# Three sums of each chunk's transform formed by accumulating DMAs, and the slab's rows in another order

## The chip, the cores and the metric

The kernel runs on one core of a Trainium2 chip. The metric is the device time of one execution in microseconds, the median of several runs. The engines are TensorE (PE; PEld is its weight load), VectorE (DVE), ScalarE (ACT), GpSimd (POOL) and SyncE (SP), which issues most DMAs. Each engine works through its own queue in order.

## The reference

A batch of 8 sequences of 3072 tokens with 256 channels goes through a convolution by FFT, then through two feed-forward layers over all 24,576 tokens.

```python
# x: (8, 3072, 256), filt_r, filt_i: (1537, 256)
X = np.fft.rfft(x, axis=1)
F = (filt_r + 1j * filt_i)[None, :, :]
y = np.fft.irfft(X * F, n=3072, axis=1)
x = y.reshape(8 * 3072, 256)
h = np.maximum(np.maximum(x @ w1, x @ w2), x @ w3)      # 768 wide
x = h @ w_out
h = x @ w_in                                            # 1024 wide
e = np.exp(h - np.max(h, -1)); sm = e / (np.sum(e, -1) + 1e-09)
solu = h * sm
ln = (solu - mean(solu)) / np.sqrt(var(solu) + 1e-06) * g_ln
return ln @ w_out2
```

## The kernel before

The work has two stages that follow each other. In stage one (to about 1640 us) the first feed-forward layer runs over the tokens of all batches, and beside it the FFT convolution of the batches that come next. In stage two the second layer runs over 192 tiles of 128 tokens; the change touches nothing there but the row number of an output.

Stage one takes 288 steps, written (b, tg, f): 8 batches, 6 groups of 512 tokens, 6 slices of 128 of the hidden layer. A step is `moe(i)`. Its `up` issues 12 matmuls of 512 columns into two PSUM banks named `h` (of four), ScalarE's `hm` (line 789), VectorE's maximum into `h` (791), ScalarE's `hh` (794) and VectorE's remainder `hl` (795). Its `down` issues the 6 matmuls of the step two back (806 to 808). Matmuls in float32r with a high and a low part stand for full precision, hence `hh` and `hl`, `xh` and `xl`.

The transform of a batch's 3072 tokens is split 24 x 128. A chunk `ch` is one half of the channels of one batch; batch 0 is done at the start in another way, and chunks 2 to 15 by a generator, `fft_stream`. A chunk lives in a slab `S[ch]`, 128 partitions (a token's place modulo 128) with 24 rows of 128 channels each, loaded by one SyncE transfer of 1536 KB in `take`. The rows are named (s, a): s one of 8, a one of 3, and stored s-major. The steps of a chunk are

- `dft8`: an 8-point transform over s for all three a, on VectorE, through a scratch tile `scr`;
- `fwd3`: a 3-point transform over a, on VectorE;
- for four groups g of rows: `fwd_in` (twiddles: ScalarE writes T from each row, line 427, 428, and VectorE combines them into U), `middle` (a 128-point transform on TensorE, the product with the filter into M on VectorE, a sum and a difference on GpSimd, line 506 and 508, a swap of halves of the partitions by two SyncE transfers, EO on VectorE) and `inv_out` (back on TensorE, twiddles on ScalarE, V in the slab on VectorE);
- `inv3` and `idft8`: the inverse transforms on VectorE. Then Y is there, and `flip` transposes it for the step that needs it.

What sets the order: the generator is advanced between the steps of `moe`. `tt` and `stt`, through which all this VectorE work goes (lines 274 and 278), add an estimate of 60 + 1.05 per element to `cost`, and after each step the loop advances the stream until `cost` has reached 3080 per step and a lead of 40000. Two more rules bind. `have` drives the stream on where the next tokens need a Y that isn't there. `free(ch)` holds chunk ch back until the last tokens of batch (ch - 5) // 2 have been flipped, since there are five slabs. The order so written is then handed to a scheduler that lays it out engine by engine; each engine keeps that order.

Of the kernel before, what the change touches and what calls it, by code (L numbers as in the profile page):

```python
# [19 lines left out]
P = 128  # L20
# [6 lines left out]

GROUPS = [(2, [15, 7, 23]), (4, [3, 19, 11]), (6, [6, 22, 14]), (0, [0, 12, 8, 20])]
N2_OF = [[(8 * a + 3 * b) % 24 for b in range(8)] for a in range(3)]


# [97 lines left out]
def kernel(ctx: ExitStack, tc: tile.TileContext, x0, xr, ff, tw, dft, first_m,  # L129
# [161 lines left out]
    def take(ch):  # L291
        j = ch % NS
        pool = yp if j in (4, 0) else fc
        S[ch] = pool.tile([P, 8, 3, P], F32, tag=f"s{j}", name="S")
        b, dc = divmod(ch, 2)
        nc.sync.dma_start(S[ch], xr[b - 1, dc])

    def scratch():
        return fc.tile([P, 30, P], F32, tag="scr", name="scr")

    def by3(v):
        return v.rearrange("p (s a) d -> p s a d", a=3)

    def dft8(ch):
        take(ch)
        O = S[ch]
        scr = scratch()
# [12 lines left out]
        yield  # L320
        h = eo[:, 0:2]
        tt(h[:, 0], eo[:, 5], eo[:, 7], ALU.subtract)
        yield
        tt(h[:, 1], eo[:, 5], eo[:, 7], ALU.add)
        yield
        stt(O[:, 2:4], h, C8, eo[:, 4:8:2])
        yield
        stt(O[:, 4:6], h, -C8, eo[:, 4:8:2])
        yield

    def idft8(ch, part=slice(0, 3)):
        b, dc = divmod(ch, 2)
        g = S[ch][:, :, part]
        scr = scratch()
        q, m = by3(scr[:, 0:24])[:, :, part], by3(scr[:, 24:30])[:, :, part]
# [82 lines left out]
    def fwd_in(ch, g):  # L418
# [615 lines left out]
    def down2(i):  # L1034
# [83 lines left out]
def _layout(x, filt_r, filt_i):  # L1118
# [60 lines left out]
```

## Time and profile before

| | |
|---|---|
| median of 3 runs | 2717.51 us (2711.11 to 2720.31) |
| the profiled execution | 2719.01 us, span 2717.2 us |
| TensorE busy | 2647.5 us, 97% |
| VectorE busy | 2256.2 us, 83% |
| ScalarE busy | 1466.7 us, 54% |
| GpSimd busy | 903.7 us, 33% |
| chain that ended last | TensorE 80%, VectorE 12%, DMA 4% |

The shares are means over two stages with different limits. A busy TensorE is not one at its peak, since its matmuls overlap and their ends are modelled; the number of instructions in a stretch tells more. "Idle before" counts the time in which an engine waited, with what released it. A line such as 274 is that of the helper `tt`; tiles and shapes tell the callers apart.

### The profile page before, as it was taken

Reading aid. Unit: us, or ns where it says so; the run is one execution under the profiler, and the core shown is the slowest. Engines: PE = TensorE matmul, PEld = TensorE weight load, DVE = VectorE, ACT = ScalarE, POOL = GpSimd, SP = SyncE. Lnnn points to the kernel's source line nnn. Section 1 sums busy time; section 2 is a strip of 40 time slices with the busy share of each in tenths; the row PEclk is TensorE's granted clock in tenths of the full one; section 3 lists DMA queues with packets and bytes.
Section 4 is the critical chain, followed back from the end, with each engine's and each line's share of the span. In section 5 each row is a group of like instructions: output and inputs, shape, how many; then the busy total and the mean of one; then the engine's idle time right before and its main releaser. Section 6 shows DMA issues by size and latency. Waiting matters only on the chain.

```text
span 2717.2 us, 38005 instructions
## 1 busy us (share of the span) xinstructions
PE 2647.5 (97%) x12096; PEld 2154.2 (79%) x12096; DVE 2256.2 (83%) x3890; ACT 1466.7 (54%) x2806; POOL 903.7 (33%) x1302
## 2 busy tenths in 40 slices
PE   6799999999999999999999999999999999999999
PEld 4478777777777777777788888888888888888888
DVE  4889999999999989989776347878878787888875
ACT  3444344444444444444344335777767777777775
POOL 0011110111110001101110003776776666767675
PEclk7899999999999999999999999999999999999999
DMA  9532323223223224232222103555555555555553
GB/s 290 167 96 75 107 58 118 72 60 118 67 81 121 61 74 119 65 94 78 77 84 87 38 24 104 145 146 151 142 145 147 143 142 138 142 145 145 141 129 90
DMA packets 172634, 300.53 MB, mean 111 GB/s; under 512 B 34289, under 2 KB 102385, under 8 KB 170449
## 3 DMA queue, kind: packets, MB, share of 16 engines
q1 hardware_dynamic: 130608, 246.01, 33.9%
q10 hardware_dynamic: 41824, 52.09, 5.9%
q8 instruction: 95, 1.56, 0.3%
q14 instruction: 107, 0.87, 0.1%
HBM read 97.95 MB, written 56.62 MB: 57 GB/s over the span
## 4 chain that ended last, share of the span: by engine, by line
PE 80%; DVE 12%; DMA 4%; issue 2%; SPq 1%; ACT 0%; POOL 0%; DVEq 0%; ACTq 0%; POOLq 0%
PE h L786 21%; PE h L969 19%; PE p L1038 13%; PE p L1040 7%; PE pf L416 5%; PE o L807 4%; PE o L808 4%; PE o L815 4%; PE o L806 3%; DVE scr L274 2%; DVE S L278 2%; DVE h L791 1%; DVE hl L795 1%; DVE M L274 1%; DVE S L274 1%
## 5 line engine op out<-in xcount | busy, mean ns | idle before, releaser
L1031 POOL TENSOR_TENSOR sl<-zt,sh 128x1024 fp32r<-128x1024 f32 x188 | 453.2, 2411 | 118.5 <-ACT sh L1030 107.8
L274 POOL TENSOR_TENSOR M<-M,M 128x384 f32<-128x384 f32 (+1 forms) x112 | 150.3, 1363 | 848.4 <-DVE M L274 734.9
L1038 PE MATMUL p<-V,sh 128*128 128x512 f32 x1536 | 380.4, 389 | 0.0
L980 DVE SCALAR_TENSOR_TENSOR sp<-h,e 128x1024 f32<-128x1024 f32 x192 | 234.1, 1219 | 159.9 <-ACT e L978 158.0
L794 ACT CAST hh<-h 128x512 fp32r<-128x512 f32 x288 | 169.6, 589 | 306.7 <-DVE h L791 295.4
L1038 PEld LDWEIGHTS p<-V,sh 128*128 128x128 f32 x1536 | 287.3, 188 | 59.3
L789 ACT ACTIVATE hm<-h 128x512 f32<-128x512 f32 x288 | 173.7, 603 | 264.7 <-PE h L786 262.9
L978 ACT ACTIVATE e<-h,sm 128x1024 f32<-128x1024 f32 x192 | 213.8, 1114 | 104.9 <-DVE sm L976 69.1
L976 DVE TENSOR_REDUCE sm<-h 128x1 f32<-128x1024 f32 x192 | 231.3, 1205 | 41.5 <-PE h L969 40.8
L1030 ACT CAST sh<-zt 128x1024 fp32r<-128x1024 f32 x188 | 196.6, 1047 | 114.5 <-PE p L1038 95.7
L982 ACT ACTIVATE e<-sp,sm 128x1024 f32<-128x1024 f32 x192 | 220.5, 1149 | 54.9 <-DVE sm L984 47.1
L791 DVE TENSOR_TENSOR h<-hm,h 128x512 f32<-128x512 f32 x288 | 196.4, 683 | 59.0 <-PE h L786 55.1
L969 PE MATMUL h<-wih,x2h 128*128 128x512 f32 x768 | 243.6, 392 | 1.2 <-ACT xo L818 1.2
L807 PE MATMUL o<-hl,woh 128*128 128x512 f32 x576 | 237.4, 412 | 5.8 <-DVE hl L795 5.8
L969 PE MATMUL h<-wih,x2l 128*128 128x512 f32 x768 | 241.6, 391 | 0.0
L969 PE MATMUL h<-wil,x2h 128*128 128x512 f32 x768 | 238.5, 390 | 0.0
L997 DVE STREAM_TRANSPOSE yt<-sp 128x1024 f32<-128x1024 f32 x188 | 231.4, 1231 | 5.0 <-issue 1.0
L806 PE MATMUL o<-hh,woh 128*128 128x512 f32 x576 | 230.2, 400 | 0.8 <-ACT hh L794 0.8
L795 DVE TENSOR_TENSOR hl<-h,hh 128x512 fp32r<-128x512 f32 x288 | 195.0, 679 | 37.9 <-ACT hh L794 37.8
L808 PE MATMUL o<-hh,wol 128*128 128x512 f32 x576 | 226.1, 393 | 0.0
L1040 PEld LDWEIGHTS p<-V,sl 128*128 128x128 f32 x1536 | 209.7, 190 | 14.9
L1040 PE MATMUL p<-V,sl 128*128 128x256 f32 x1536 | 214.9, 282 | 0.0
(167 smaller groups left out, 5626.1 us busy)
## 6 DMA issues: line engine op xcount, KB each, us to landing
zt<-yt SPq DMA_DIRECT2D x752, 128.0 KB, 2.6
x<-xo SPq DMA_DIRECT2D x96, 256.0 KB, 2.2
x<-x ACTq DMA_DIRECT2D x48, 512.0 KB, 3.6
S<-in_xr_dram SPq DMA_DIRECT2D x14, 1536.0 KB, 7.9
out_dram<-ob ACTq DMA_DIRECT2D x168, 128.0 KB, 2.2
zt<-yt SPq DMA_DIRECT2D x640, 32.0 KB, 1.9
F<-in_ff_dram SPq DMA_DIRECT2D x48, 384.0 KB, 3.4
F<-in_ff_dram SPq DMA_DIRECT2D x16, 512.0 KB, 3.9
```

The costliest lines, as they stand in the source:

```text
L274: return eng.tensor_tensor(o, a, b, op=op)
L786: nc.tensor.matmul(ph[j], wt[:, c, f * P:(f + 1) * P], xt[:, c], start=i == 0, stop=i == 5)
L806: nc.tensor.matmul(po[m], wo_h[:, f, cs], hh, start=f == 0, stop=False)
L807: nc.tensor.matmul(po[m], wo_h[:, f, cs], hl, start=False, stop=False)
L808: nc.tensor.matmul(po[m], wo_l[:, f, cs], hh, start=False, stop=False)
L969: nc.tensor.matmul(h[:, fs], xt[:, c, ts], wt[:, c, fs], start=n == 0, stop=n == 5)
L976: nc.vector.tensor_reduce(sm[:, 0:1], h, axis=AX.X, op=ALU.max, negate=True)
L980: nc.vector.scalar_tensor_tensor(sp, h, 1.0, e, op0=ALU.mult, op1=ALU.mult, accum_out=sm[:, 2:3])
L997: nc.vector.transpose(out=YT[g][:, :, t].rearrange("p j c k -> p c j k"), in_=sp.rearrange("p (c j k) -> p c j k", c=NF2, j=4))
L1031: nc.gpsimd.tensor_tensor(lv, z, hv, op=ALU.subtract)
L1038: nc.tensor.matmul(p, sh[:, c], V2[:, c], start=c == 0, stop=False)
L1040: nc.tensor.matmul(p[:, :D], sl[:, c], V2[:, c, :D], start=False, stop=c == NF2 - 1)
```

## The change

Three sums are no longer VectorE instructions but transfers that add to what lies in the slab, issued from GpSimd's queue by a new helper `add_in`:

- in `dft8`, the sum of rows s = 0 to 3 and 4 to 7 (1536 elements per partition): rows 4 to 7 are read from the input in DRAM a second time and added into rows 0 to 3. VectorE forms the difference first, odd rows and even rows apart, since the transfer overwrites what it reads, then the part that needs only the differences, then the part that needs the sums;
- in `fwd3`, r[:, :, 0] + s (1024 elements): s lies in a tile of its own, `sac`, and is added into the slab's rows a = 0;
- in `inv3`, the same for 768 elements.

The slab is now stored a-major (`t` with 3 x 8 rows, seen as (s, a)), so that the accumulated rows lie side by side, the input is laid out to match, and the eight rows of the 8-point transform stand in another order: the pairs of a group lie at 4, 6, 2 and 0, and the output rows are found through `Y_AT`. In `fwd_in` the row j = 0, on which the transfer lands, is taken last. `idft8` has as many instructions of the same sizes as before. The filter tables keep their order, as the groups keep theirs.

```diff
-GROUPS = [(2, [15, 7, 23]), (4, [3, 19, 11]), (6, [6, 22, 14]), (0, [0, 12, 8, 20])]
+GROUPS = [(4, [15, 7, 23]), (6, [3, 19, 11]), (2, [6, 22, 14]), (0, [0, 12, 8, 20])]
+Y_AT = [0, 2, 4, 6, 5, 7, 1, 3]
...
-        S[ch] = pool.tile([P, 8, 3, P], F32, tag=f"s{j}", name="S")
+        t = pool.tile([P, 3, 8, P], F32, tag=f"s{j}", name="S")
+        S[ch] = t.rearrange("p a s d -> p s a d")
         b, dc = divmod(ch, 2)
-        nc.sync.dma_start(S[ch], xr[b - 1, dc])
+        nc.sync.dma_start(t, xr[b - 1, dc])
 
     def scratch():
-        return fc.tile([P, 30, P], F32, tag="scr", name="scr")
+        return fc.tile([P, 18, P], F32, tag="scr", name="scr")
+
+    def addend():
+        return fc.tile([P, 8, P], F32, tag="sac", name="sac")
+
+    def add_in(o, a):
+        nc.gpsimd.dma_start(o, a, accum_op=ALU.add)
...
     def dft8(ch):
         take(ch)
         O = S[ch]
-        eo, f = by3(scr[:, 0:24]), by3(scr[:, 24:30])
-        tt(eo[:, 0:4], O[:, 0:4], O[:, 4:8], ALU.add)
-        yield
-        tt(eo[:, 4:8], O[:, 0:4], O[:, 4:8], ALU.subtract)
-        yield
-        tt(f[:, 0:2], eo[:, 0:2], eo[:, 2:4], ALU.add)
-        yield
-        tt(O[:, 6:8], eo[:, 0:2], eo[:, 2:4], ALU.subtract)
+        odd, h = by3(scr[:, 0:12]), by3(scr[:, 12:18])
+        tt(odd[:, 2:4], O[:, 1:4:2], O[:, 5:8:2], ALU.subtract)
+        yield
+        tt(odd[:, 0:2], O[:, 0:4:2], O[:, 4:8:2], ALU.subtract)
+        add_in(O[:, 0:4].rearrange("p s a d -> p a s d"), xr[b - 1, dc][:, :, 4:8])
+        yield
+        tt(h[:, 0], odd[:, 2], odd[:, 3], ALU.subtract)
+        yield
+        tt(h[:, 1], odd[:, 2], odd[:, 3], ALU.add)
+        yield
+        stt(two(O[:, 4:6]), two(h), C8, two(odd[:, 0:2]))
+        yield
+        stt(two(O[:, 6:8]), two(h), -C8, two(odd[:, 0:2]))
+        yield
+        f = odd[:, 2:4]
+        tt(f, O[:, 0:2], O[:, 2:4], ALU.add)
+        yield
+        tt(O[:, 2:4], O[:, 0:2], O[:, 2:4], ALU.subtract)
...
@@ fwd3
-        s, d, t = scr[:, 0:8], scr[:, 8:14], scr[:, 14:20]
+        s, d, t = addend(), scr[:, 0:6], scr[:, 6:12]
...
         stt(t, s[:, 2:8], -0.5, r[:, 2:8, 0])
-        yield
-        tt(r[:, :, 0], r[:, :, 0], s, ALU.add)
+        add_in(r[:, :, 0], s)
         yield
...
@@ inv3
-        s, d, t, t0 = scr[:, 0:6], scr[:, 6:12], scr[:, 12:18], scr[:, 18:20]
+        s, d, t, t0 = addend()[:, 0:6], scr[:, 0:6], scr[:, 6:12], scr[:, 12:14]
         tt(s, v[:, 2:8, 1], v[:, 2:8, 2], ALU.add)
         yield
+        stt(t, s, -0.5, v[:, 2:8, 0])
+        add_in(v[:, 2:8, 0], s)
+        yield
         tt(d, v[:, 2:8, 1], v[:, 2:8, 2], ALU.subtract)
-        yield
-        stt(t, s, -0.5, v[:, 2:8, 0])
-        yield
-        tt(v[:, 2:8, 0], v[:, 2:8, 0], s, ALU.add)
         yield
...
@@ fwd_in
-            for j, k in enumerate(ks):
+            for j, k in order(ks):
...
+    def order(ks):
+        return list(enumerate(ks))[1:] + [(0, ks[0])]
```

How the order of instructions changes shows best at chunk 5, the first that meets a full load of VectorE. VectorE before, from the two instructions of 1536 (sum and difference) that open its `dft8`:

```order
L274 TENSOR_TENSOR scr<-S 128x1536 x2
L791 TENSOR_TENSOR h<-hm,h 128x512
L274 TENSOR_TENSOR M_2289<-Z,F 128x768
L274 TENSOR_TENSOR M_2274<-swap,F 128x768
L274 TENSOR_TENSOR scr<-scr 128x768
L791 TENSOR_TENSOR h<-hm,h 128x512
L274 TENSOR_TENSOR S<-scr 128x768
L278 SCALAR_TENSOR_TENSOR S<-pf,tws,T_2281 128x2x128 x3
L795 TENSOR_TENSOR hl<-h,hh 128x512
L770 TENSOR_TENSOR xl<-h,xh 128x512
L274 TENSOR_TENSOR S<-scr 128x384 x2
L770 TENSOR_TENSOR xl<-h,xh 128x512
```

VectorE now, from the product that stands ahead to the first reader of the accumulated rows, the last `scr<-S` (f); line 805 is the maximum `h`, 809 the remainder `hl`, 275 and 279 the helpers, 784 `xl`:

```order
L275 TENSOR_TENSOR M_2586<-Z,F 128x1024
L275 TENSOR_TENSOR scr<-S 128x2x3x128 x2
L275 TENSOR_TENSOR M_2541<-swap,F 128x1024
L809 TENSOR_TENSOR hl<-h,hh 128x512
L805 TENSOR_TENSOR h<-hm,h 128x512
L275 TENSOR_TENSOR scr<-scr 128x3x128 x2
L279 SCALAR_TENSOR_TENSOR S<-pf,tws,T_2577 128x256 x3
L279 SCALAR_TENSOR_TENSOR S<-scr 128x3x256 x2
L784 TENSOR_TENSOR xl<-h,xh 128x512
L809 TENSOR_TENSOR hl<-h,hh 128x512
L275 TENSOR_TENSOR scr<-S 128x2x3x128
```

The two of 1536 have become two of 768; the sums' part of the transform, which came right behind them, now stands behind the differences' part and behind work of other steps. GpSimd before, from the end of that chunk's neighbourhood on; M1 and M2 are the products of `middle`, S the slabs by number:

```order
L274 TENSOR_TENSOR M1_2915<-M1_2915,M2_2871 128x384 x2
L274 TENSOR_TENSOR M1_3153<-M1_3153,M2_3107 128x384 x2
L274 TENSOR_TENSOR M1_3299<-M1_3299,M2_3284 128x384 x2
L274 TENSOR_TENSOR M1_3440<-M1_3440,M2_3425 128x512 x2
L274 TENSOR_TENSOR M1_3682<-M1_3682,M2_3606 128x384 x2
L437 MEMSET U_3908 128x128
L274 TENSOR_TENSOR M1_3834<-M1_3834,M2_3782 128x384 x2
```

GpSimd now, a similar piece; 307 is `add_in`:

```order
L275 TENSOR_TENSOR M1_2776<-M1_2776,M2_2738 128x384 x2
L307 DMA S_1454<-sac_2694 128x768
L275 TENSOR_TENSOR M1_3021<-M1_3021,M2_2973 128x384 x2
L275 TENSOR_TENSOR M1_3198<-M1_3198,M2_3183 128x384 x2
L307 DMA S_2446<-sac_2981 128x1024
L275 TENSOR_TENSOR M1_3306<-M1_3306,M2_3258 128x512 x2
L307 DMA S_2384<-sac_3398 128x768
L275 TENSOR_TENSOR M1_3519<-M1_3519,M2_3480 128x384 x2
L448 MEMSET U_3781 128x128
L275 TENSOR_TENSOR M1_3669<-M1_3669,M2_3623 128x384 x2
L307 DMA S_4041<-in_xr_dram 128x3x512
```

Three transfers per chunk stand between the pairs, in one queue with them. ScalarE before, at the twiddles of chunk 5's group 0 (T from S_2376; 789 is `hm`, 794 `hh`):

```order
L789 ACTIVATE hm_2717<-h_2703 128x512
L794 CAST hh_2689<-h_2673 128x512
L428 ACTIVATE T_2528<-S_2376,tws_135 128x128
L427 ACTIVATE T_2528<-S_2376,tws_135 128x128 x2
L428 ACTIVATE T_2528<-S_2376,tws_135 128x128
L427 ACTIVATE T_2528<-S_2376,tws_135 128x128
L428 ACTIVATE T_2528<-S_2376,tws_135 128x128
```

ScalarE now (S_2384; 803 is `hm`, 808 `hh`):

```order
L439 ACTIVATE T_2438<-S_2384,tws_135 128x128
L438 ACTIVATE T_2438<-S_2384,tws_135 128x128 x2
L439 ACTIVATE T_2438<-S_2384,tws_135 128x128
L803 ACTIVATE hm_2910<-h_2896 128x512
L808 CAST hh_2873<-h_2857 128x512
L438 ACTIVATE T_2438<-S_2384,tws_135 128x128
L439 ACTIVATE T_2438<-S_2384,tws_135 128x128
L803 ACTIVATE hm_2951<-h_2937 128x512
L808 CAST hh_2913<-h_2897 128x512
L438 ACTIVATE T_2685<-S_2384,tws_135 128x128
```

The twiddles of row 0, the last 438 and 439 of T_2438, come behind a step's `hm` and `hh`, and the next step's stand behind them.

## Rows read from the trace of the kernel before

**Rows 1.** Stretches of the run; columns as the first line names them.

```profile
core 0: us, PE busy (x) PEld busy (x) DVE busy (x) ACT busy (x) POOL busy (x), PEclk, DMA share, GB/s
300.00:380.00 80.00, 73.40 (x296) 55.84 (x295) 75.86 (x125) 32.93 (x81) 7.97 (x6) 0.96 0.33 100
380.00:500.00 120.00, 118.50 (x497) 92.92 (x496) 118.94 (x203) 53.16 (x128) 16.54 (x14) 1.00 0.34 101
500.00:580.00 80.00, 74.77 (x304) 58.01 (x303) 80.00 (x127) 33.75 (x82) 8.36 (x7) 0.96 0.21 58
580.00:1220.00 640.00, 633.48 (x2655) 497.56 (x2655) 611.98 (x983) 290.60 (x694) 77.05 (x63) 1.00 0.31 88
1220.00:1380.00 160.00, 160.00 (x676) 126.47 (x675) 144.05 (x237) 69.22 (x164) 17.44 (x15) 1.00 0.25 69
1380.00:1500.00 120.00, 120.00 (x530) 99.09 (x529) 73.81 (x125) 54.16 (x94) 16.88 (x12) 1.00 0.32 96
```

**Rows 2.** Chain that ended last, around 300 us: start us, us, what.

```profile
...
300.27 11.98 DMA S<-in_xr_dram
...
313.45 0.60 SPq L746
...
322.27 1.15 DVE EO L278 x2
...
```

**Rows 3.** VectorE in order of time, around 330 us: start us, busy us, instruction.

```profile
329.87 3.40 DVE L274 TENSOR_TENSOR scr<-S 128x1536 f32<-128x1536 f32 x2
333.19 0.68 DVE L791 TENSOR_TENSOR h<-hm,h 128x512 f32<-128x512 f32 x1
333.79 0.95 DVE L274 TENSOR_TENSOR M<-Z,F 128x768 f32<-128x768 f32 x1
334.65 0.95 DVE L274 TENSOR_TENSOR M<-swap,F 128x768 f32<-128x768 f32 x1
...
338.06 1.26 DVE L278 SCALAR_TENSOR_TENSOR S<-pf,tws,T 128x256 f32<-128x256 f32 x3
...
342.57 1.01 DVE L274 TENSOR_TENSOR scr<-scr 128x384 f32<-128x384 f32 x2
...
344.56 1.81 DVE L278 SCALAR_TENSOR_TENSOR S<-scr 128x768 f32<-128x768 f32 x2
```

**Rows 4.** VectorE by line and shape, 136 to 1650 us: busy us, mean ns.

```profile
L274 DVE TENSOR_TENSOR scr<-S 128x768 f32<-128x768 f32 x63 | 61.0, 985 | 0.0
...
L274 DVE TENSOR_TENSOR scr<-S 128x1536 f32<-128x1536 f32 x26 | 46.5, 1827 | 1.8 <-DMA S<-in_xr_dram 1.8
...
L274 DVE TENSOR_TENSOR M<-Z,F 128x1024 f32<-128x1024 f32 x14 | 17.0, 1212 | 0.1
```

**Rows 5.** VectorE by line and shape: 300 to 580 us, then 580 to 1220.

```profile
L274 DVE TENSOR_TENSOR scr<-S 128x1536 f32<-128x1536 f32 x8 | 14.7, 1879 | 0.0
L274 DVE TENSOR_TENSOR S<-S,scr 128x1024 f32<-128x1024 f32 x3 | 3.6, 1210 | 0.0
L274 DVE TENSOR_TENSOR S<-S,scr 128x768 f32<-128x768 f32 x3 | 2.8, 942 | 0.0
...
L274 DVE TENSOR_TENSOR scr<-S 128x1536 f32<-128x1536 f32 x12 | 21.5, 1832 | 0.0
L274 DVE TENSOR_TENSOR S<-S,scr 128x1024 f32<-128x1024 f32 x7 | 8.5, 1209 | 0.0
L274 DVE TENSOR_TENSOR S<-S,scr 128x768 f32<-128x768 f32 x7 | 6.6, 947 | 0.0
```

**Rows 6.** DMA issues: out<-in, queue, count, KB each, median us to landing.

```profile
S<-in_xr_dram SPq DMA_DIRECT2D x14, 1536.0 KB, 7.9
...
F<-in_ff_dram SPq DMA_DIRECT2D x16, 512.0 KB, 3.9
...
xb<-in_x_dram SPq DMA_DIRECT2D x1, 1152.0 KB, 13.3
```

**Rows 7.** GpSimd by line and shape, 136 to 1650 us: busy us, mean ns, idle before.

```profile
L274 POOL TENSOR_TENSOR M<-M,M 128x384 f32<-128x384 f32 x84 | 111.1, 1344 | 590.2 <-DVE M L274 508.3 <-ACT hm L789 65.4 <-ACT hh L794 16.5
```

More of the change, by code (lines that the diff above doesn't have):

```diff
@@ L293, in take, with two @@
         pool = yp if j in (4, 0) else fc
-        S[ch] = pool.tile([P, 8, 3, P], F32, tag=f"s{j}", name="S")
+        t = pool.tile([P, 3, 8, P], F32, tag=f"s{j}", name="S")
+        S[ch] = t.rearrange("p a s d -> p s a d")
         b, dc = divmod(ch, 2)
-        nc.sync.dma_start(S[ch], xr[b - 1, dc])
+        nc.sync.dma_start(t, xr[b - 1, dc])
     def scratch():
-        return fc.tile([P, 30, P], F32, tag="scr", name="scr")
+        return fc.tile([P, 18, P], F32, tag="scr", name="scr")
[3 more added lines that the diff above has]
+        nc.gpsimd.dma_start(o, a, accum_op=ALU.add)
     def by3(v):
-        return v.rearrange("p (s a) d -> p s a d", a=3)
+        return v.rearrange("p (a s) d -> p s a d", a=3)
+    def two(v):
+        return v.rearrange("p s a d -> p a s d")
     def dft8(ch):
@@ L306, in dft8 @@
         O = S[ch]
+        b, dc = divmod(ch, 2)
         scr = scratch()
-        eo, f = by3(scr[:, 0:24]), by3(scr[:, 24:30])
-        tt(eo[:, 0:4], O[:, 0:4], O[:, 4:8], ALU.add)
+        odd, h = by3(scr[:, 0:12]), by3(scr[:, 12:18])
+        tt(odd[:, 2:4], O[:, 1:4:2], O[:, 5:8:2], ALU.subtract)
         yield
-        tt(eo[:, 4:8], O[:, 0:4], O[:, 4:8], ALU.subtract)
+        tt(odd[:, 0:2], O[:, 0:4:2], O[:, 4:8:2], ALU.subtract)
+        add_in(O[:, 0:4].rearrange("p s a d -> p a s d"), xr[b - 1, dc][:, :, 4:8])
         yield
-        tt(f[:, 0:2], eo[:, 0:2], eo[:, 2:4], ALU.add)
+        tt(h[:, 0], odd[:, 2], odd[:, 3], ALU.subtract)
         yield
-        tt(O[:, 6:8], eo[:, 0:2], eo[:, 2:4], ALU.subtract)
+        tt(h[:, 1], odd[:, 2], odd[:, 3], ALU.add)
[8 more added lines that the diff above has]
+        tt(O[:, 2:4], O[:, 0:2], O[:, 2:4], ALU.subtract)
         yield
@@ L320, in dft8 @@
         yield
-        h = eo[:, 0:2]
-        tt(h[:, 0], eo[:, 5], eo[:, 7], ALU.subtract)
-        yield
-        tt(h[:, 1], eo[:, 5], eo[:, 7], ALU.add)
-        yield
-        stt(O[:, 2:4], h, C8, eo[:, 4:8:2])
-        yield
-        stt(O[:, 4:6], h, -C8, eo[:, 4:8:2])
-        yield
     def idft8(ch, part=slice(0, 3)):
@@ L334, in idft8 @@
         scr = scratch()
-        q, m = by3(scr[:, 0:24])[:, :, part], by3(scr[:, 24:30])[:, :, part]
+        w, m = by3(scr[:, 0:12])[:, :, part], by3(scr[:, 12:18])[:, :, part]
         tt(m[:, 0], g[:, 0], g[:, 1], ALU.add)
@@ L339, in idft8 @@
         yield
-        tt(q[:, 0:2], m[:, 0:2], g[:, 6:8], ALU.add)
+        tt(w[:, 0:4:2], m, g[:, 2:4], ALU.add)
         yield
-        tt(q[:, 2:4], m[:, 0:2], g[:, 6:8], ALU.subtract)
+        tt(w[:, 1:4:2], m, g[:, 2:4], ALU.subtract)
         yield
-        tt(m[:, 0:2], g[:, 2:4], g[:, 4:6], ALU.subtract)
+        tt(m, g[:, 4:6], g[:, 6:8], ALU.subtract)
         yield
-        tt(q[:, 4:6], g[:, 2:4], g[:, 4:6], ALU.add)
+        tt(g[:, 4:6], g[:, 4:6], g[:, 6:8], ALU.add)
         yield
-        tt(q[:, 6], m[:, 0], m[:, 1], ALU.add)
+        tt(g[:, 6], m[:, 0], m[:, 1], ALU.add)
         yield
-        tt(q[:, 7], m[:, 1], m[:, 0], ALU.subtract)
+        tt(g[:, 7], m[:, 1], m[:, 0], ALU.subtract)
         yield
-        tt(g[:, 0:4:2], q[:, 0:4:2], q[:, 4:6], ALU.add)
+        tt(g[:, 0:2], w[:, 0:2], g[:, 4:6], ALU.add)
         yield
-        tt(g[:, 4:8:2], q[:, 0:4:2], q[:, 4:6], ALU.subtract)
+        tt(g[:, 2:4], w[:, 0:2], g[:, 4:6], ALU.subtract)
         yield
-        stt(g[:, 1:4:2], q[:, 6:8], C8, q[:, 1:4:2])
+        stt(two(g[:, 4:6]), two(g[:, 6:8]), -C8, two(w[:, 2:4]))
         yield
-        stt(g[:, 5:8:2], q[:, 6:8], -C8, q[:, 1:4:2])
+        stt(two(g[:, 6:8]), two(g[:, 6:8]), C8, two(w[:, 2:4]))
         for a in range(3)[part]:
@@ L428, in fwd_in @@
                 nc.scalar.activation(T[:, 2 * j + 1], x[:, 0], AF.Copy, scale=col("ns", k))
-            for j, k in enumerate(ks):
+            for j, k in order(ks):
                 stt(U[:, j:j + 4:3], X[:, sl:sl + 2, j], col("c", k), T[:, 2 * j:2 * j + 2])
@@ L1055, in down2 @@
         a, hf = divmod(tg, 2)
-        row = b * SEQ + N2_OF[a][hf * 4 + j] * P
+        row = b * SEQ + N2_OF[a][Y_AT[hf * 4 + j]] * P
         nc.scalar.dma_start(out[row:row + P], ob)
@@ L1122, in _layout @@
     xr = x[1:].reshape(B - 1, N2, P, 2, P)[:, order]
-    xr = xr.reshape(B - 1, 3, 8, P, 2, P).transpose(0, 4, 3, 2, 1, 5)
+    xr = xr.reshape(B - 1, 3, 8, P, 2, P).transpose(0, 4, 3, 1, 2, 5)
     xr = np.ascontiguousarray(xr)
```

1 line of the change is left out of this document (removed).

## The prediction

> **What bounds the kernel now.** I read the stretches of the whole run first. The reader is to see in [rows 1] that TensorE is busy nearly all the time from 300 us on, and that its instruction count tells more than its busy time: from 1220 to 1380 it gets through 676 matmuls in 160 us, 4.225 per us, with no idle time and with the transform's matmuls still among them. I take that as TensorE's own pace. At that pace 300 to 580 us (three rows, 280 us) would hold 1183 matmuls; the rows hold 296 + 497 + 304 = 1097, so 86 are missing, 86 / 4.225 = 20.4 us. 580 to 1220 would hold 2704 and holds 2655: 49 missing, 11.6 us. What TensorE lost there is the most that a lighter VectorE can give back: 32 us. From 1220 on there is nothing to win: TensorE is never idle there while VectorE is at 144.05 of 160 us and then, from 1380, at 73.81 of 120; the last stage, after it, has TensorE busy throughout in the page's slices as well.
>
> The same rows name the other side. VectorE is busy 274.8 of 280 us in 300 to 580, and 611.98 of 640 in 580 to 1220. So the first of these stretches is VectorE's, with TensorE close behind, and the second is nearly balanced. In the two worst slices the granted clock of TensorE also falls, to 0.96, which is a mean over its two levels of 2.4 and 1.2 GHz; a filled gap would win that back too, and the count above holds it already.
>
> Not all of the loss is VectorE's work. The chain around 300 us [rows 2] runs through the 1536 KB load of a slab, which took 11.98 us there, and through SyncE's queue, where each small transfer behind it takes 0.6 us to issue, to a swap that released the EO step only at 322 us. No VectorE instruction that is taken away here would shorten that.
>
> **What the change removes.** Per chunk, three sums leave VectorE. In dft8 two instructions of 1536 elements become two of 768: the pair took 3.32 us from its start to the start of what follows (329.87 to 333.19), and one of 768 takes 0.86 (333.79 to 334.65) [rows 3], so 3.32 - 2 x 0.865 = 1.59 us go. I use starts and not the mean durations of [rows 4] (1827 and 985 ns), because neighbours overlap by about 0.08 us. In fwd3 a sum of 1024 goes, 1210 ns less that overlap, 1.13 us; in inv3 one of 768, 942 ns, 0.87 us [rows 5]. Together 3.59 us per chunk and 14 chunks.
>
> Does the pace table take it back? The emission loop counts estimated VectorE cost, and the change lowers a chunk's count. But a slab comes free only when the tokens of an earlier batch are flipped, and in the orders of both kernels the chunks start at nearly the same steps (counted by the rows of h that stand ahead in VectorE's order: chunk 5 at step 33 before and 34 now, the last at 200 and 199). So the same transform work still belongs to the same steps, and the load per step falls. By [rows 5] the stretch from 300 to 580 holds 4 dft8, 3 fwd3 and 3 inv3: 4 x 1.59 + 3 x 1.13 + 3 x 0.87 = 12.4 us leave VectorE. The one from 580 to 1220 holds 6, 7 and 7: 23.5 us.
>
> **What it adds.** Each removed sum becomes an accumulating transfer on GpSimd's queue, and its reader must wait for the landing. The trace has no such transfer, so I bound it. From below: 768 KB as a plain load lies between 512 KB at 3.9 us and 1536 KB at 7.9 us [rows 6], 4.9 us. From above: the slowest comparable load, 1152 KB at 13.3 us beside other loads. I take 7.9 us: a sum has two operands, so 768 KB of result means 1536 KB to be read, and that is the slab load's row; with 0.6 us for the issue, as a row of SyncE's queue shows, 8.5 us.
>
> The Trainium skill, "Collectives: The Full Stack", section "The bandwidth ceiling: the fold count and why AG ≠ RS ≠ AR", speaks against the change in the same way: a reducing transfer reads two sources through one ring and delivers about half of what a copy does. By that rule the sum stays at the 7.9 us row; without it, it would be 4.9 us. No run here shows an accumulating transfer yet.
>
> Against it stands the cover. In dft8 of chunk 5 the first reader of the accumulated rows (the sum f) stands behind these instructions after the second subtraction: a product of 1024 (1.13 us), hl and h (0.6 each), two of 384 (1.01 for the pair, less the overlap 0.93), three of 256 (1.18), two of 768 (1.73), xl and hl (0.6 each, like h), 7.4 us by [rows 3, 4]. 8.5 - 7.4 leaves VectorE waiting 1.1 us per chunk; behind the waiting f in its queue stand xl, EO, h and hl, for which TensorE waits if it lasts longer than the two steps of lead that four PSUM banks give. Other chunks have a similar cover, the last two some 2 to 3 us less. The bounds give a wait of 0 (landing after 5.5 us) to 6.5 us (13.9 us).
>
> The second transfer (fwd3, 512 KB) is waited for first by ScalarE: the twiddle of row 0, moved behind the two other rows. It blocks hm and hh behind it in ScalarE's queue. By the same doubling it lands like 1024 KB, between 3.9 and 7.9, say 5.9 us plus the issue, and VectorE reads what depends on it 6.8 us of its own work later at the nearest place. ScalarE is busy 53.16 of 120 us [rows 1], so I cost it at nothing; without that cover it would be the same few us per chunk. The third (inv3, 384 KB) is read by idft8 behind six own instructions and what is interleaved, over 10 us, or frees the shared addend, which is written 5.5 us later or more: nothing. GpSimd's own pairs of sums are unchanged (1344 ns each [rows 7]), and it sat idle 590 us before them; in its new order no transfer stands ahead of a pair that is ready earlier, so issuing costs nothing, at worst one pair's 1.4 us of delay to a swap. The second reading of half a slab and the two transfers inside SBUF add traffic to DMA engines that are busy a third of the time [rows 1]: nothing, or a few tenths per swap. The new row order leaves the number and size of all other VectorE instructions alone. A 768 that reads strided rows costs 985 ns, one that does not 947 [rows 4, 5]: up to 45 ns either way on some dozen instructions a chunk, 0.5 us per chunk, taken as nothing and kept in the range.
>
> **The sum.** From 300 to 580 VectorE is relieved of 12.4 us and given 4 x 1.1 of waiting: 8.0 us net. As it is the bound in most of that stretch, but not in the chain of [rows 2], I count two thirds, 5.3 us. From 580 to 1220 it is 23.5 - 6 x 1.1 = 16.9 us, of which I count a third, 5.6 us, half of what TensorE lost there. Before 300 and after 1220 nothing. Together 11 us: 2719.0 us, the profiled execution, becomes 2708. The median of the runs lies 1.5 us under that execution, so I predict 2707 us.
>
> **Rivals.**
> 1. *The transfer is slow and becomes the wait.* If it lands at the upper bound, 13.9 us after the subtraction, VectorE stands 6.5 us per dft8: 4 x 6.5 - 12.4 = +14 us in the first stretch, all on the path, and 6 x 6.5 - 23.5 = +15 in the second, against 28 us of idle VectorE, so half, +8. 2719 + 22 = 2741. It decides from a landing of 7.4 + 12.4 / 4 = 10.5 us on. For it: slab loads have taken up to 11.98 us, and pairs of them are issued back to back just where the sums start. Against it: the median of 7.9.
> 2. *The removed work is not what TensorE lacked.* If the two gaps come from slab loads and SyncE's queue, as the chain at 300 us shows, less work only makes VectorE wait longer for the same releases: a gain of 0 to 6 us, 2716. Against it: VectorE is busy 80.00 of 80 us from 500 to 580.
> 3. *Everything hides.* If the sum lands like a plain load, no wait appears, and the stretches give 12.4 and at most 11.6 us: 2695. For it: only a third of the DMA time is in use.
> 4. *The change does not take the load off*, since a planner orders anew, and queues (SyncE's above all) come out differently in places: plus or minus 5 us around any of these, inside the ranges.
>
> **Chances and range.** Forecast (gain of 8 to 20 us) 0.37; everything hides 0.09; no difference 0.27; slow transfer 0.27. A measurement of this kernel tells 0.3% from no change, 8 us. That gives faster 0.45, within 0.3% 0.29, slower 0.26. The likeliest case has 2698 to 2711 as its own range. With the other cases it reaches from 2693 (rival 3 against the median) to 2739 (rival 1 against the median).
>
> **What would show it.** Right: VectorE's busy time falls by 14 x 3.6, about 50 us; the rows of 1536 and the sums S<-S,scr are gone; the wait of dft8's f for a transfer is around 1 us each; from 300 to 580 the matmul count rises above 1097 and its clock above 0.96. The forecast is wrong if the landing of the 768 KB transfer is over 10.5 us or ScalarE's twiddle waits hold up hm; then VectorE's idle time grows under a DMA releaser and the counts fall. It is wrong the other way if the 580 to 1220 stretch reaches TensorE's own pace.

## The result and the profile after

The changed kernel takes 2731.98 us (median of 5 runs, 2728.92 to 2733.11) against 2715.86 for the kernel before (2711.11 to 2720.31): ratio 1.0057, 95% interval 1.0043 to 1.0072. It is 16 us slower, where 11 us of gain were forecast. The profiled span is 2731.0 us.

The stretches of the changed kernel, in the columns of [rows 1], which they answer:

```profile
300.00:380.00 80.00, 75.25 (x324) 58.88 (x323) 74.08 (x123) 31.65 (x76) 10.19 (x9) 0.98 0.46 122
380.00:500.00 120.00, 120.00 (x505) 94.31 (x504) 117.86 (x209) 55.22 (x135) 19.05 (x17) 1.00 0.42 114
500.00:580.00 80.00, 73.06 (x298) 55.83 (x297) 75.97 (x125) 34.43 (x87) 14.01 (x12) 0.98 0.39 87
580.00:1220.00 640.00, 630.78 (x2637) 493.97 (x2636) 586.07 (x976) 288.56 (x693) 100.48 (x85) 1.00 0.40 105
1220.00:1380.00 160.00, 156.46 (x657) 122.61 (x656) 132.54 (x217) 65.35 (x153) 17.21 (x17) 1.00 0.33 86
1380.00:1500.00 120.00, 118.60 (x521) 97.13 (x520) 71.56 (x121) 52.16 (x90) 15.83 (x12) 1.00 0.29 88
```

VectorE is lighter in every row, by 12 of 160 us even from 1220 to 1380, and TensorE gets through fewer matmuls in four of the six: 657 for 676 from 1220 to 1380, where the prediction had nothing to be won. Only 300 to 500 gained. Over the whole span VectorE's busy time fell from 2256.2 to 2203.0 us, as forecast. So the load left VectorE, and the time went up.

How a wait travels is seen at the last chunk's dft8, the longest of eight such waits. VectorE in order of time (start, busy, instruction, and in brackets the idle time ahead of it), answering [rows 3]:

```profile
1230.18 1.81 DVE L275 TENSOR_TENSOR scr<-S 128x768 f32<-128x768 f32 x2
1231.92 0.69 DVE L805 TENSOR_TENSOR h<-hm,h 128x512 f32<-128x512 f32 x1
1232.51 1.02 DVE L275 TENSOR_TENSOR scr<-scr 128x384 f32<-128x384 f32 x2
1233.45 0.69 DVE L809 TENSOR_TENSOR hl<-h,hh 128x512 fp32r<-128x512 f32 x1
1234.05 1.82 DVE L279 SCALAR_TENSOR_TENSOR S<-scr 128x768 f32<-128x768 f32 x2
1241.29 0.96 DVE L275 TENSOR_TENSOR scr<-S 128x768 f32<-128x768 f32 x1 [5.42 <-DMA S<-in_xr_dram]
1242.16 1.29 DVE L774 TENSOR_TENSOR xl<-zt,xh 128x512 fp32r<-128x512 f32 x2
1243.37 0.95 DVE L275 TENSOR_TENSOR S<-S 128x768 f32<-128x768 f32 x1
1244.24 0.69 DVE L805 TENSOR_TENSOR h<-hm,h 128x512 f32<-128x512 f32 x1
```

The two subtractions of 768 end at 1232; f, which reads the landed sum, stands behind six more instructions and starts at 1241.29 after 5.42 us of waiting. The h of the MoE step stands behind f. Its wait goes on to ScalarE and from there to TensorE, in the same view:

```profile
1244.96 0.58 ACT L808 CAST hh<-h 128x512 fp32r<-128x512 f32 x1 [6.56 <-DVE h L805]
...
1245.60 0.50 PE L820 MATMUL o<-hh,woh 128*128 128x512 f32 x1 [1.10 <-ACT hh L808]
```

TensorE still had other matmuls to run while f waited, so it stood still for 1.10 us at this place, not for 5.42.

The chain that ended last runs through this transfer here (start us, us, what), as the chain of [rows 2] ran through a slab load:

```profile
1232.30 8.97 DMA S<-in_xr_dram
...
1241.29 0.03 DVE scr L275
```

The transfers of the changed kernel (KB each, median us to landing), answering [rows 6]:

```profile
S<-in_xr_dram SPq DMA_DIRECT2D x14, 1536.0 KB, 7.4
...
F<-in_ff_dram SPq DMA_DIRECT2D x16, 512.0 KB, 4.3
...
S<-in_xr_dram POOLq DMA_DIRECT2D x14, 768.0 KB, 8.5
...
S<-sac POOLq DMA_DIRECT2D x14, 512.0 KB, 5.6
S<-sac POOLq DMA_DIRECT2D x14, 384.0 KB, 4.1
```

And who waited for them, by the line that issues all three (us in all, times), with VectorE's group of that shape ([rows 4]):

```profile
  ACT T L438: 28.7, 14
  DVE scr L275: 21.1, 8
  DVE sac L275: 2.3, 1
```

```profile
L275 DVE TENSOR_TENSOR scr<-S 128x768 f32<-128x768 f32 x77 | 75.4, 994 | 26.5 <-DMA S<-in_xr_dram 26.5
```

GpSimd's own pairs of sums hardly changed, 1263 ns where [rows 7] have 1344:

```profile
L275 POOL TENSOR_TENSOR M<-M,M 128x384 f32<-128x384 f32 x84 | 104.4, 1263 | 474.6 <-DVE M L275 453.1 <-ACT T L572 10.8 <-ACT th L244 7.4
```

VectorE waited 26.5 us for slabs in front of that shape, 21.1 of them in 8 waits for the accumulating transfer; ScalarE's twiddles (T) waited 28.7 us in 14.

### The profile page after: what moved, and what is told of

It is laid out like the page before. It is cut to its first block, busy times and chain, and to the rows that moved or that the text cites. A ratio compares the mean times of both kernels' runs of the same rounds, so it can differ in the third digit from the quotient of the medians.

```text
span 2731.0 us, 38141 instructions
## 1 busy us (share of the span) xinstructions
PE 2649.9 (97%) x12096; PEld 2151.9 (79%) x12096; DVE 2203.0 (81%) x3862; ACT 1462.9 (54%) x2806; POOL 939.7 (34%) x1344
## 4 chain that ended last, share of the span: by engine, by line
PE 51%; DMA 1%; DVE 1%; SPq 1%; issue 0%; POOL 0%; ACT 0%; DVEq 0%; ACTq 0%; POOLq 0%
PE h L983 19%; PE p L1052 13%; PE h L800 7%; PE p L1054 7%; PE o L829 1%; PE o L821 1%; PE o L822 1%; PE o L820 1%; SPq L760 1%; PE pf L427 0%; DMA raw<-in_w_in_dram 0%; DMA S<-in_xr_dram 0%; DMA raw<-in_w_out_dram 0%; DVE h L805 0%; DMA zt<-yt 0%
## 5 line engine op out<-in xcount | busy, mean ns | idle before, releaser
L994 DVE SCALAR_TENSOR_TENSOR sp<-h,e 128x1024 f32<-128x1024 f32 x192 | 234.2, 1220 | 159.7 <-ACT e L992 157.8
L1011 DVE STREAM_TRANSPOSE yt<-sp 128x1024 f32<-128x1024 f32 x188 | 231.5, 1232 | 4.2
```

Source lines behind the costliest of these rows:

```text
L994: nc.vector.scalar_tensor_tensor(sp, h, 1.0, e, op0=ALU.mult, op1=ALU.mult, accum_out=sm[:, 2:3])
L1011: nc.vector.transpose(out=YT[g][:, :, t].rearrange("p j c k -> p c j k"), in_=sp.rearrange("p (c j k) -> p c j k", c=NF2, j=4))
```

## The experiments

Theory 1: the price is f's wait for dft8's transfer, at the head of VectorE's queue. Theory 2: it is ScalarE's wait for the two others. Theory 3: it is the added traffic. Theory 4: it is the new row order and the new order of instructions. "Layout kernel" means the changed kernel with all three sums on VectorE. The brackets hold the 95% interval of the ratio to the kernel before, run in turn on the same chip.

### Each part alone

```
e1  - add_in(O[:, 0:4]..., xr...)          + tt(O[:, 0:4], O[:, 0:4], O[:, 4:8], ALU.add)
e2  - add_in(r[:, :, 0], s)                + tt(r[:, :, 0], r[:, :, 0], s, ALU.add)
    - add_in(v[:, 2:8, 0], s)              + tt(v[:, 2:8, 0], v[:, 2:8, 0], s, ALU.add)
e3  both of these
e6  e3, with add_in(v[:, 2:8, 0], s) kept
```

Dft8's sum back on VectorE (e1): 

> The changed kernel with the sum of dft8 back on VectorE (one instruction of 1536 elements, in place); the accumulating transfers of fwd3 and inv3 stay, and so does the new row order. Before 2716, changed 2732. Theory 1 (the wait of f for the 768 KB landing, 21 us in 8 waits at the head of VectorE's queue with h and hl behind it, is what costs): most of the 16 us comes back, 2714 to 2720, and VectorE's waits for S<-in_xr are gone. Theory 2 (the 512 and 384 KB transfers cost, by ScalarE's 28.7 us of waiting for them in front of the twiddles): 2728 or more, ScalarE's waits unchanged. Theory 4 (row order and re-planned order alone): 2728 or more as well, told from theory 2 by the layout kernel.

Measured 2709.88 [0.9973, 0.9991], 22 us under the changed kernel and below theory 1's range; theories 2 and 4 expected 2728 or more. VectorE still waits 5.0 us for S<-in_xr, for the slab loads themselves.

Only dft8's as a transfer (e2): 

> The counterpart: only dft8's sum is an accumulating transfer, those of fwd3 and inv3 are on VectorE. Theory 1: 2726 to 2736, as slow as the changed kernel, waits for S<-in_xr of 15 to 25 us on VectorE. Theory 2: 2712 to 2720, ScalarE's waits for S<-sac gone. Theory 3 (the added traffic delays the swaps, EO and M wait 17 us longer in all): in between, since 768 of the 1664 KB per chunk remain.

Measured 2717.36 [1.0004, 1.0022]; VectorE waits 16.8 us for that transfer in 9 waits. The waits are those of theory 1, but the time lies in theory 2's range: measured against the kernel before, this run speaks against theory 1. The next run shows why that was the wrong yardstick.

No transfer (e3): 

> Row order and layout of the changed kernel, but all three sums on VectorE: no accumulating transfer at all. Theories 1, 2 and 3: about before, 2712 to 2722, VectorE's busy time back to 2250 to 2256 us. Theory 4 (the new row order and the re-planned queues cost by themselves): 2728 or more.

Measured 2703.82 [0.9948, 0.9973], VectorE's busy time 2252.3 us. Every theory missed this: the layout alone, which relieves VectorE of next to nothing (before has 2256.2), is 11 us faster than before. Measured from it, the transfers cost far more than 16 us: fwd3's and inv3's 6, dft8's 13.5, all three 28.

Only inv3's as a transfer (e6): 

> The layout kernel (2704) with only inv3's sum as an accumulating transfer (384 KB); dft8 and fwd3 on VectorE. Its reader stands over 10 us later. If a hidden transfer is free and VectorE's relief (14 x 0.87 = 12 us) counts for something: 2698 to 2703. If the relief is worth nothing: 2702 to 2706. If each transfer costs by the way it delays others (theory 3) or by the re-planned order: 2706 to 2712.

Measured 2708.73 [0.9970, 0.9987], 5 us over the layout kernel. That is in the size of what another order of the same work moves (below), so it shows no more than that the 12 us of relief did not appear.

### The transfer itself, in an unchanged order

The next three kernels have every instruction of every engine where the changed kernel has it; only the adding is taken from a transfer, so that it lands sooner.

```
e5   - nc.gpsimd.dma_start(o, a, accum_op=ALU.add)   + nc.gpsimd.dma_start(o, a)
e10  the same in dft8 alone          e11  the same in fwd3 and inv3 alone
```

All three plain (e5): 

> The changed kernel with its three transfers as plain copies to the same places on the same queue, nothing added (the three sums are left out of the result); every instruction of every engine stands where it stood. If an accumulating transfer reads two sources and pays for both, the plain 768 KB lands in 5 to 6 us and not in 8.5; then f hardly waits (under 8 us in all), and by theory 1 the time falls from 2732 to 2712 to 2720. If the landing stays at 8 us or more, adding is free and the time stays at 2728 to 2734. If the landing shrinks and the time doesn't, the waits for transfers are not what costs, and the order is.

Measured 2709.29 [0.9970, 0.9988], below theory 1's range. VectorE's waits for dft8's transfer fell from 21.1 us to 5.6. The landings of e5:

```profile
S<-in_xr_dram POOLq DMA_DIRECT2D x14, 768.0 KB, 5.8
...
S<-sac POOLq DMA_DIRECT2D x14, 512.0 KB, 3.2
S<-sac POOLq DMA_DIRECT2D x14, 384.0 KB, 2.7
```

Only dft8's plain (e10): 

> The changed kernel (2732) in its own order; only dft8's transfer is a plain copy (its sum is left out), those of fwd3 and inv3 still add. With all three plain it was 2709, 23 us less: f's waits fell by 15.1 us, ScalarE's T waits by 19.2. Theory 1 (f's wait is the price): 15 to 22 us less, 2710 to 2717. Theory 2 (ScalarE's T wait is the price): 0 to 8 us less, 2724 to 2732.

Measured 2713.80 [0.9984, 1.0002]: 18 of the 23 us. VectorE's waits for this transfer fell from 21.1 us to 6.3, while its waits for slabs in all fell from 26.5 to 12.3. The last chunk of e10, VectorE in order of time, in the columns of the same place above:

```profile
1219.91 1.82 DVE L279 SCALAR_TENSOR_TENSOR S<-scr 128x768 f32<-128x768 f32 x2
1224.46 0.96 DVE L275 TENSOR_TENSOR scr<-S 128x768 f32<-128x768 f32 x1 [2.72 <-DMA S<-in_xr_dram]
```

The same f, behind the same instructions, waits 2.72 us and not 5.42.

Only the two others plain (e11): 

> The counterpart in the same order: dft8's transfer adds, the two others are plain copies (their sums are left out). Theory 1: 0 to 8 us less, 2724 to 2732. Theory 2: 15 to 22 us less, 2710 to 2717. If both cost: the two gains sum to about 23.

Measured 2730.97 [1.0041, 1.0066]: 1 us. Theory 2 falls as the main price, and with it ScalarE's longer list of waits: ScalarE waited 19 us less, and the time hardly moved. Theory 1 holds for most of the 23 us. Over e10, e5 is another 4.5 us faster, so the two small transfers seem to cost something only once the large one no longer does; with different chips under the two runs, that is not certain.

### The reader later

```
e4   def dft8: f and the three behind it become dft8b, which stages() runs after idft8 of the
     chunk before; else: with tc.issue_after(HL[-3]): tt(f, O[:, 0:2], O[:, 2:4], ALU.add)
```

> All three transfers as in the changed kernel, but the readers of dft8's landed rows (f and what follows) stand later in VectorE's order: behind idft8 of the chunk before where the order allows it (some 50 us of own work between trigger and f), else behind the hl of a later MoE step (10.9 us or more of own work, from chunk 8 on; chunks 5 and 7 keep 6.9 and 6.6). Theory 1: the waits for S<-in_xr fall from 26 us to under 8, and the time to 2716 to 2724. Theory 2 and theory 3: the waits fall too, but the time stays at 2728 to 2734. If later rows only push the chunk's next steps late, it is above 2732.

Measured 2710.75 [0.9977, 0.9995], with 11.1 us of waiting for S<-in_xr instead of 26.5 (theory 1 said under 8); 6.0 of them are for the transfer. The direction is theory 1's; the gain, 21 us, is more than it forecast, presumably since the edit also gives everything around f another order. Even so it stays 7 us over the layout kernel: a transfer that is mostly hidden still did not beat having none.

### Traffic without a reader

```
e8   e3 + nc.gpsimd.dma_start(SPARE[:, :n], xr[b - 1, dc][:, 0, :n], accum_op=ALU.add)   (3 places)
```

> The layout kernel (2704), all sums on VectorE, with three accumulating transfers per chunk issued at the same places (512, 512 and 384 KB from HBM) into a spare tile that nobody reads: traffic and GpSimd issues without any wait for them. Theory 3 (traffic delays swaps and loads): EO's wait for swaps rises from 11.5 to 20 us or more, and the time to 2710 to 2718. Theory 1 (only waits for the landing cost): 2702 to 2706.

Measured 2790.42 [1.0264, 1.0292], and it tells nothing of theory 3. With nothing to wait for, the 42 transfers were all issued by 295 us, and as they share one tile, GpSimd waited for its own. Which work that held up, and so where the 75 us come from, was not followed (us, times, longest):

```profile
POOL spare L316 <- DMA spare<-in_xr_dram: 231.2, 40, 11.8
```

Theory 3 has better evidence against it elsewhere. EO's waits for a swap were 25.0 us in the changed kernel and 24.1 in e5, with nothing added in the transfers and 23 us less time. These waits are longer than the layout kernel's 11.5, but e12 (below), which has no such transfer at all and the same work on VectorE, has 22.8: they come with a lighter VectorE, and the traffic isn't needed for them. The swap<-M itself lands in 3.0 us (median) in the changed kernel and in 2.9 in the layout kernel.

### The order, and what relief is worth

```
e9   before, PACE 3080 -> 3050               e13  e3, PACE 3050
e12  the changed kernel without the three add_in (sums left out)       e18  e12, PACE 3050
e14  e3, the odd half as tt(odd, O[:, 0:4], O[:, 4:8], ALU.subtract)
e15  e3, s = scr[:, 18:26] of one scratch of 26 rows                   e19  e15, PACE 3050
e16  e3, f and the three behind it ahead of h
```

The pace of the kernel before (e9): 

> A control: the kernel before with the pace of its emission loop at 3050 instead of 3080, which gives VectorE, ScalarE and TensorE another order (some 500 to 900 rows differ) and changes no work. If a re-planned order alone moves the time by several us, it shows here: theory 4 says 2705 to 2725, at least 5 us from 2715. If orders of the same work are alike: 2713 to 2718.

Measured 2717.49 [1.0003, 1.0021]: 3 us by order alone.

The pace of the layout kernel (e13): 

> A second control: the layout kernel (2704) with the pace at 3050 instead of 3080. If the layout's gain of 11 us is its own, the time stays at 2701 to 2708; if it is one lucky order of many, it goes to 2709 to 2718.

Measured 2704.90 [0.9946, 0.9970]: the layout's 11 us hold in a second order.

No sums at all (e12, then e18 in a second order): 

> The changed kernel with the three sums neither on VectorE nor as transfers: they are left out. It shows the most that relieving VectorE of them can bring, 53 us of its busy time, without any price. If VectorE's load is what TensorE lacked (the prediction): 2685 to 2697, since TensorE's counts of the layout kernel (2704) leave 78 matmuls or 18 us to win between 300 and 1220. If the relief is worth nothing (rival 2 of the prediction): 2700 to 2710.

Measured 2705.66 [0.9952, 0.9972], which reads as no worth at all. 

> The kernel without the three sums (they are left out; 2706 at a pace of 3080) in another order, at a pace of 3050. If relieving VectorE of 53 us is worth nothing over the layout kernel (2704 and 2705 at the two paces), and 2706 was no unlucky order: 2700 to 2710. If it hid a gain: 2688 to 2698.

Measured 2692.84 [0.9899, 0.9926]. This turns e12's verdict round. Two orders of the same work are 13 us apart. In the slower one TensorE has three waits of over 2 us for hl, which the other hasn't (start, busy, and in brackets the wait; the execution shown took 2710 us, 5 us over the median):

```profile
336.57 0.74 PE L797 MATMUL h<-xh,w0h 128*128 128x512 f32 x2 [2.14 <-DVE hl L806]
...
530.49 1.22 PE L797 MATMUL h<-xh,w0h 128*128 128x512 f32 x2 [3.39 <-DVE hl L806]
...
1054.54 0.67 PE L818 MATMUL o<-hl,woh 128*128 128x512 f32 x1 [3.85 <-DVE hl L806]
```

So 53 us of relief, free of any price, are worth between nothing and 12 us over the layout kernel (2704 and 2705 in its two orders), by the order that comes with them.

Which part of the layout gives its 11 us? The odd half as one block (e14): 

> The layout kernel (2704) with the odd half of dft8 as one instruction of 1536 elements next to the sum of 1536, as before had it: 3.4 us of VectorE in one block in front of h. If the layout's 11 us come from breaking up that block: 2710 to 2716. If not: 2701 to 2707.

One scratch (e15): 

> The layout kernel (2704) with the addend of fwd3 and inv3 again in the one scratch buffer that all four transforms share (26 rows), as before. If the second buffer, by which a transform can start before the one ahead of it has let go of the scratch, is what gave the 11 us: 2710 to 2716. If not: 2701 to 2707.

The even half first (e16): 

> The layout kernel (2704) with dft8's even half (f and the three that follow) ahead of the odd half's h, as before had it. If the order of the halves gave the 11 us: 2710 to 2716. If not: 2701 to 2707. If all three of these kernels stay at 2701 to 2707, the gain lies in the in-place inverse transform or in the sum of small things.

Measured 2703.61 [0.9953, 0.9978], 2697.14 [0.9923, 0.9950] and 2706.29 [0.9957, 0.9980]. None loses the gain, so none of the three parts alone is its source; and without the second scratch buffer the kernel is 7 us faster still. In a second order, e19: 

> The layout kernel with one scratch buffer (2697, the fastest so far) at a pace of 3050. If the 7 us over the layout kernel belong to the one scratch: 2694 to 2700. If they belong to one good order: 2701 to 2707.

Measured 2695.30 [0.9910, 0.9935]. The layout with one scratch and no transfer is the fastest kernel here that computes everything, 20 us under before and 37 under the changed kernel.

### One edge in the kernel before

The traces of the layout kernels lack two stalls that before has: between 300 and 580 us TensorE waits over 2 us at a time twice in before and twice in its other order (e9, 4.42 and 3.90 us, and a time no better), and never in the layout kernel, e13, e14, e15, e16 and e19. TensorE in before (start, busy, and the wait in brackets), and the stretches around them:

```profile
339.46 2.04 PE L416 MATMUL pf<-U,df 128*128 128x512 f32 x2 [4.42 <-DVE S L278]
...
540.51 0.80 PE L786 MATMUL h<-xh,w0h 128*128 128x512 f32 x1 [3.92 <-DVE hl L795]
```

```profile
330.00:340.00 10.00, 4.74 (x21) 3.30 (x20) 10.00 (x13) 3.81 (x10) 3.26 (x2) 0.91 0.30 83
340.00:350.00 10.00, 10.00 (x31) 6.72 (x30) 10.00 (x16) 1.52 (x3) 0.00 (x0) 0.75 0.13 29
530.00:540.00 10.00, 6.58 (x32) 4.88 (x30) 10.00 (x10) 3.98 (x12) 2.82 (x2) 0.98 0.26 66
540.00:550.00 10.00, 9.49 (x30) 7.59 (x31) 10.00 (x19) 5.11 (x15) 0.00 (x0) 0.68 0.00 0
```

At the prediction's pace of 4.225 per us these four stretches would hold 169 matmuls; they hold 114. So 55 of the 86 that it found missing between 300 and 580 are missing in two places. The first is in [rows 3]: TensorE waits for the three S<-pf at 338.06, which stand behind the pair of 1536, h, two products and the two of 768. At the second it is again a pair of 1536, 4.50 us long, with a U and the hl behind it:

```profile
534.96 4.50 DVE L274 TENSOR_TENSOR scr<-S 128x1536 f32<-128x1536 f32 x2
539.38 0.47 DVE L278 SCALAR_TENSOR_TENSOR U<-S,tws,T 128x256 f32<-128x256 f32 x1
539.78 0.68 DVE L795 TENSOR_TENSOR hl<-h,hh 128x512 fp32r<-128x512 f32 x1
```

So one rule of order was added to before, at chunk 5, and nothing else:

```diff
-        tt(eo[:, 0:4], O[:, 0:4], O[:, 4:8], ALU.add)
+        with tc.issue_after(VL[-1]) if ch == 5 else nullcontext():   # VL: the last S<-pf
+            tt(eo[:, 0:4], O[:, 0:4], O[:, 4:8], ALU.add)
```

> The kernel before (2715) with one added rule of order and nothing else: the sum of chunk 5's dft8 stands behind the S<-pf that lets TensorE's pair bank go, so that one of the two instructions of 1536 elements and the two of 768 behind it no longer stand ahead of it. If VectorE's order at this place and not the amount of its work cost TensorE there (4.42 us of waiting at 335 us, and a granted clock of 0.75 in the 10 us after it): the stall is gone or under 1.5 us, the clock at 340 to 350 us is 1.00, and the time is 2706 to 2711. If the stall only moves to another place: 2713 to 2717.

Measured 2704.51 [0.9947, 0.9974]: 10 us less, 1.5 us below the range named, and VectorE's busy time is 2255.2 us, as before. VectorE of this kernel at the place, and its stretches:

```profile
326.80 1.74 DVE L274 TENSOR_TENSOR scr<-S 128x1536 f32<-128x1536 f32 x1
...
331.99 1.26 DVE L278 SCALAR_TENSOR_TENSOR S<-pf,tws,T 128x256 f32<-128x256 f32 x3
333.17 1.75 DVE L274 TENSOR_TENSOR scr<-S 128x1536 f32<-128x1536 f32 x1
```

```profile
330.00:340.00 10.00, 8.74 (x38) 6.35 (x37) 9.23 (x15) 4.08 (x11) 1.96 (x2) 1.00 0.26 75
340.00:350.00 10.00, 10.00 (x44) 7.93 (x43) 10.00 (x16) 4.52 (x11) 2.25 (x1) 1.00 0.24 60
530.00:540.00 10.00, 9.77 (x44) 7.74 (x43) 10.00 (x16) 5.36 (x13) 0.16 (x1) 1.00 0.10 26
540.00:550.00 10.00, 10.00 (x43) 7.76 (x42) 10.00 (x21) 6.71 (x20) 0.00 (x0) 1.00 0.22 71
```

The count of these four is 169 for 114, and the clock stays at its upper level. Over 300 to 580 as one stretch, before and then this kernel:

```profile
300.00:580.00 280.00, 266.66 (x1095) 206.77 (x1094) 274.79 (x453) 119.83 (x290) 32.87 (x27) 0.98 0.30 88
300.00:580.00 280.00, 277.13 (x1169) 217.52 (x1169) 273.27 (x460) 127.57 (x306) 33.68 (x28) 1.00 0.30 89
```

Both stalls are gone, the second because everything behind chunk 5 was ordered anew; how much each was worth was not separated. A pair of 1536 is not a stall by itself: in this kernel one still stands ahead of two hl, from 537.62 us on and 3.42 us long, and TensorE does not wait 2 us there. What counts is whether the release behind it was due. Not all that was won is kept: 74 matmuls more by 580 us would be 17.5 us, and from 580 to 1220 this kernel has 2640 where before has 2655.

## Why the prediction was wrong

- **Ceiling, right.** 20 us were missing between 300 and 580, and the one edge brought the 1095 matmuls there to 1169, of 1183 at TensorE's pace.
- **What would win it back, wrong.** This step failed first: "As it is the bound in most of that stretch ... I count two thirds". A VectorE that is busy 274.8 of 280 us [rows 1] was read as a load that TensorE waits for. Most of the loss, 55 of 86 matmuls, was two waits of 4 us with the slow clock behind them, each for one release that stood behind other work of VectorE, 8 us of it (329.87 to 338.06) and 5 us (534.96 to 539.78). The layout kernel and the edge won 10 to 11 us with the load unchanged; taking the whole load off won 0 to 12 us on top, where two thirds of 12.4 and a third of 23.5 would be 16.
- **Row order and re-planning at nothing, wrong.** The sum has no term for them ("The new row order leaves the number and size of all other VectorE instructions alone"). The layout is worth -11 us, and nothing in the prediction forecast it. Rival 4 gave re-planned orders 5 us either way; two orders of one kernel were 3 us apart in before, 1 in the layout kernel and 13 in the kernel without sums.
- **Landing, right as a median, in part by luck.** 7.9 + 0.6 = 8.5 us was forecast and 8.5 measured. But the 7.9 of the slab load already counts from its issue, so the 0.6 was counted twice; GpSimd's own issue takes 1.18 us. And a median hides the spread: at the odd chunks from 3 on the transfer took 8.0 to 10.6 us, at the even ones from 4 on 6.9 to 7.4. A plain copy at the same place took 5.8 for 8.5 us, 3.2 for 5.6 and 2.7 for 4.1, so adding made the landing 1.5 to 1.75 times as long. The Trainium skill, "Collectives: The Full Stack", section "The bandwidth ceiling: the fold count and why AG ≠ RS ≠ AR", states of a collective that a reduce step, which reads two sources, delivers about half of a copy's rate. The runs here agree with it in direction, with less than a factor of two.
- **The wait, too small, and its price by far.** This step turned the sign. 1.1 us per dft8 were forecast, which is 11 us over the ten chunks of the sum; 21.1 us were measured over the whole run, in 8 waits. Seven of them stand at the odd chunks, and one, of 0.2 us, at an even one: at the odd chunks the transfer landed later, and their cover shrank from one to the next. Between the end of the second subtraction and the moment at which f would have been next lie 9.3 us at chunk 5, 7.1 at chunk 7, 5.1 at chunk 13 and 3.9 at chunk 15 (the prediction had 7.4, "the last two some 2 to 3 us less", and then used 1.1 for all). At chunk 5 the wait came out at 1.38 us, close to the 1.1, but by luck: cover and landing (10.1 us) were both longer than assumed. The step "4 x 1.1 of waiting ... net" then subtracted the wait from the relief, us by us, and counted two thirds and a third of the rest, so that all waits together cost 5 us in its sum. Measured, dft8's transfer cost 13.5 us over the layout kernel by itself, and in the changed kernel's own order taking 14 us off VectorE's waits for slabs (26.5 to 12.3 in e10) took 18 off the time. That a wait costs more than its own length, because it is a block in front of h, while relief is spread thin, is the reading that fits; it was not tested apart.
- **ScalarE's wait at nothing, about right**: in the changed kernel's order 19 us less of it were worth 1 us (e11). **Inv3's transfer at nothing**: open; e6 has it alone and is 5 us over the layout kernel, which another order could be. **GpSimd at nothing, right**: in the trace of the changed kernel no pair of its sums that stands behind a transfer starts more than 0.3 us after its products.
- **Rival 1** forecast a slowdown for this reason, with a wait of the right place, but let it decide only "from a landing of 7.4 + 12.4 / 4 = 10.5 us on", from the same trade of wait against relief. The waits decided at a median of 8.5. **Rival 2** was largely right that the removed work is not what TensorE lacked (0 to 12 us), and wrong on where the gaps come from: not from slab loads and SyncE's queue, but from VectorE's order.
- The signs named ahead came out split: VectorE's busy time, the gone shapes, and a count over 1097 with a clock over 0.96 from 300 to 580, all as in the right case; and idle time under a DMA releaser with falling counts from 500 on, as in the wrong one, although the landing stayed under the 10.5 us named for it.

Summed from the layout kernel: -11 for the layout, +13.5 for dft8's transfer, +6 for the other two, +8.5 when they meet, makes +16 to 17. The 8.5 are the remainder; what they are made of stays open, and so does theory 3 as a small part. What made the layout's 11 us is shown only so far: the two stalls are gone, and taking them out of before by one edge is worth about as much; which part of the layout moved them is open.

## What to carry to other kernels

Before a busy share is called a bound, look for the few longest waits of the engine that is to be fed and read what stands ahead of each release in the other engine's queue: one edge may be worth as much as all the work removed. A wait put at the head of an in-order queue is priced by what stands behind it, chunk by chunk with each one's own cover and landing, and is not to be netted against work removed elsewhere. And where every edit re-plans the order, run one kernel in a second order before reading a difference of a few us as the edit's.

## What was not expected of the hardware

- Adding in a transfer cost 1.4 to 2.7 us of landing over a plain copy of the same bytes at the same place, and GpSimd's own instruction grew too: 1177 ns against 774 for 768 KB, 884 against 568 for the smaller two.
- A TensorE wait of some 4 us was followed by a granted clock of 0.75 and 0.68 over the next 10 us, a mean over 2.4 and 1.2 GHz: 31 and 30 matmuls where 43 or 44 stand in each 10 us from 350 to 380. Of the 55 matmuls missing around the two stalls 23 are missing in these two stretches, after the waits, and 23 at 4.225 per us are 5.4 us, beside 8.3 us of waits.
